# Chunk attention and a gated feed-forward layer: the order of two groups of loads, and the PSUM tiles of the wide units' values

## The chip, the core and the metric

The kernel runs on one core of one Trainium2 chip. The metric is the device time of one execution in microseconds (us). The engines meant below are PE (matmul), DVE (vector), ACT (activations and copies; its queue also issues the stores), POOL (element-wise work; its queue issues nearly all loads) and SP (a DMA queue). Each takes its own instructions strictly in the order in which they were written, and waits for the others through semaphores.

## The reference, cut to what matters

Inputs q, k, v are [8 batches, 8 heads, 576 tokens, 64]. Each 64-token chunk attends to itself; the result, taken as 4608 tokens of width 512, goes through a layer of width 2048 with a gate and back to 512.

```python
scores = (1 / sqrt(64)) * q_c @ k_c.T          # per batch, head and chunk of 64 tokens
attn = exp(scores - max(scores)); attn /= sum(attn) + 1e-9
x = (attn @ v_c)  ->  [4608, 512]
h = x @ w_in                                   # w_in: 512 x 2048
g = h * (1 / (1 + exp(-beta * h)))
out = g @ w_out                                # w_out: 2048 x 512
```

## The kernel before

**Attention, in units.** A batch has nine chunks. Batch 0 is cut into units 0 and 1 of four chunks each (the *wide* units; their loads are laid out differently) and unit 2, the last chunk alone. Every later batch has three units of three chunks: units 3, 4, 5 are batch 1, units 6, 7, 8 batch 2, and so on. For each unit: DVE transposes q and k in blocks (qt, kt; L197, L206), PE makes the scores (s, L249), DVE takes the maximum and subtracts it (mx L261, sh L270), ACT the exponential (ex L278), DVE sums and inverts (sum L289, ri L293), DVE or, from unit 7 on, POOL normalises (pn L305, L311), PE transposes the result (pt L325; from unit 9 on a DMA does) and ACT copies it out (et L333), PE multiplies by v (xa, L353; wide units L365), and ACT writes the result, transposed, into XT in SBUF (L376). For a wide unit this last copy is split: ACT takes one half (r = 0, L384), DVE the other (r = 1, L386). A wide unit's v goes through a selection on PE first (va, L218) and a copy by ACT (vv, L229).

**Feed-forward.** Tokens are taken in blocks of 512, the first three of them cut into pieces (256 + 256, 256 + 256, 320 + 192). A *hidden group* is four matmuls into one PSUM bank (hps, L399), 16 groups a piece; ACT takes the tanh (sg, L411) and DVE the gate (gt, L417). An *output group* is four matmuls with one of the four pieces of w_out (ops, L427), four groups to 128 tokens, accumulated in one bank; ACT copies the sum (osb, L437) and issues its store. A piece's hidden groups need the XT of all its tokens; output groups take the pieces of w_out in order.

**PSUM.** One two-bank tile for scores (`ps_s`), one two-bank tile for values and half of the selection (`ps_x`), and four one-bank tiles (`ps_p`) shared by hidden groups, output groups, transposes and the other half of the selection.

**Order.** A planner in the kernel writes the order of every engine's instructions. It holds a list of tasks with an engine, an estimated length, predecessors and buffers taken and given, and always emits the task that it thinks can start first, hidden and output groups with a small handicap. A task list entry says which buffers a task takes, so changing it changes the order everywhere behind it. The loads stand in a fixed order, `LOADS`, on POOL's queue; those of the third batch on follow in order of the units. A load of a batch's q, k or v (L153, L158) is eight DMAs, one per head; a "last" load (L124, L128) fetches the last chunk of batch 0, two DMAs for q, two for k and four for v; each piece of w_out is one DMA (L168). Batch 1 is loaded in two parts, its first three chunks (unit 3) and the other six (units 4 and 5). The DMAs on POOL's queue use eight semaphores in turn.

Of the kernel before, what the change touches and what calls it, by code (L numbers as in the profile page):

```python
# [8 lines left out]
FP32 = mybir.dt.float32  # L9
# [7 lines left out]
def kernel(  # L17
# [25 lines left out]
    CH = 64  # L43
    NCH = S // CH
    KDM = DM // 128
# [138 lines left out]
    sc, pr, et, xa = {}, {}, {}, {}  # L184
# [156 lines left out]
    def values(u):  # L341


        b, c0, n, grp = units[u]
        x = et.pop(u)
        a = ps_x.tile([128, 2, 512], FP32, tag="x", name="xa")
        if grp is None:
            f = raw["v", b].rearrange("p (c y s d) -> p c y s d", c=NCH, y=2, s=2)
            for c in range(n):
                for y in range(2):  # L350
                    for s in range(2):
                        for g in range(2):
                            nc.tensor.matmul(  # L353
                                out=a[64 * s:64 * s + 64, g, (y * n + c) * CH:(y * n + c + 1) * CH],
                                lhsT=f[64 * g:64 * g + 64, c0 + c, y, s, :],
                                rhs=x[64 * g:64 * g + 64, 2 * c + s, 64 * y:64 * y + 64],
                                start=True, stop=True)
        else:
            for g in range(2):
                for y in range(2):  # L360
                    for c in range(2):
                        for s in range(2):
                            for r in range(2):
                                o = ((2 * y + g) * 2 + c) * CH
                                nc.tensor.matmul(  # L365
                                    out=a[64 * s:64 * s + 64, r, o:o + CH],
                                    lhsT=tr["v", b, grp][64 * r:64 * r + 64, 2 * g + s, c, y, :],
                                    rhs=x[64 * r:64 * r + 64, 4 * g + 2 * s + c, 64 * y:64 * y + 64],
                                    start=True, stop=True)
        xa[u] = a  # L370

    def put(u, r=None):
        b, c0, n, grp = units[u]
        t0, w = b * S + c0 * CH, n * CH
        if grp is None:
            nc.scalar.activation(  # L376
                out=XT[:, :, t0:t0 + w].rearrange("p (y g) t -> p g y t", g=2),
                in_=xa.pop(u)[:, :, 0:2 * w].rearrange("p g (y t) -> p g y t", y=2),
                func=ACTF.Copy)
            return  # L380
        o = XT[:, :, t0:t0 + w].rearrange("p k (c r t) -> p k c r t", c=2, r=2)[:, :, :, r]
        i = xa[u][:, r].rearrange("p (k c t) -> p k c t", k=KDM, c=2)
        if r == 0:
            nc.scalar.activation(out=o, in_=i, func=ACTF.Copy)  # L384
        else:
            nc.vector.tensor_copy(out=o, in_=i)  # L386
# [77 lines left out]
    def task(eng, length, fn, *args, after=(), ready=0.0, take=(), give=(), lag=0.0, load=None, kind="a", behind=None):  # L464
        i = len(tasks)
        tasks.append(dict(eng=eng, len=length, fn=fn, args=args, after=[x for x in after if x is not None],
                          ready=ready, take=take, give=give, lag=lag, load=load, kind=kind, end=None))
        if behind is not None:
            order.append((behind, i))
        return i  # L470

    def dve(n):
        return 0.15 + n * 0.00105

    def act(n):
        return 0.2 + n * 0.00082
# [6 lines left out]
    AHEAD, LAZY = 9999, 1.0  # L483
    TRACE = None
    LOADS = [("k", 0, 0), ("v", 0, 0), "ident", ("q", 0, 1), ("k", 0, 1), ("v", 0, 1), ("w_in", 0), ("w_in", 1),
             ("w_out", 0), ("last", "q"), ("last", "k"), ("last", "v"), ("w_out", 1), ("w_out", 2), ("w_out", 3),
             ("q", 1), ("k", 1), ("v", 1), ("q", 1, 1, 1), ("k", 1, 1, 1), ("v", 1, 1, 1)]
    PARTS = {1: [(0, 0, 3), (1, 3, 6)]}
    PIECES = {0: [(0, 256, 0, 16), (256, 256, 0, 16)], 1: [(0, 256, 0, 16), (256, 256, 0, 16)],
              2: [(0, 320, 0, 16), (320, 192, 0, 16)]}  # L490
# [54 lines left out]
    put_of, norm_of = {}, {}  # L545
# [14 lines left out]
    for u in range(NU):  # L560
        b, c0, n, grp = units[u]
        e = n * 256
        if b > 1 and u == first[b]:
            for name in "qkv":
                for p, _, _ in PARTS.get(b, [(0, 0, 9)]):
                    pair(name, b, p)
        part = c0 // 4 if b in WIDE else max(p for p, c1, _ in PARTS.get(b, [(0, 0, 9)]) if c1 <= c0)
        for name in "qk":
            length = dve(512) if grp is not None else dve(e // 2) + 0.05
            if (b, part) == (0, 0):  # L570
                x = [task("DVE", dve(256), turn, name, 0, (i,), take=(name + "t",) if i == 0 else (),
                          after=[cast_q[i] if name == "q" else loaded["k", 0, 0]]) for i in range(2)]
                turned[name, u] = x
                last_turn[name, b] = x[1]
            else:
                x = task("DVE", length, turn, name, u, take=(name + "t",), after=[loaded[name, b, part]])
                turned[name, u] = [x]
                last_turn[name, b] = x
        if grp is not None:
            x = task("PE", 1.1, select, b, grp, after=[loaded["v", b, part], sel_in], take=("p", "p", "x"))  # L580
            copied[u] = []
            for g in range(4):
                copied[u].append(task("ACT", act(256), select_copy, b, grp, g, after=[x] + copied[u][:1],
                                      take=("vv",) if g == 0 else (), give=("x",) if g == 1 else ("p",) if g > 1 else ()))
        tq = turned["q", u] + turned["k", u]
        before = [tasks_of[u - 1]] if u else []
        length = 0.2 + 0.13 * n
        if u >= FUSE:
            w = u - LAG
            nw = units[w][2]  # L590
            x = task("PE", length + 0.02 + 0.065 * nw, lambda u=u, w=w: (values(w), scores(u)), kind="v",
                     after=tq + before + ready_for[w], take=("s", "x"), give=("qt", "kt") + values_give[w])
            value_of[w] = x
        else:
            x = task("PE", length, scores, u, after=tq + before, take=("s",), give=("qt", "kt"))
        tasks_of[u] = x
        score = x
        flips = []
        for gs in ((0,), (1,)) if u in SPLIT else ((0, 1),):
            k = len(gs)  # L600
            h = e * k // 2
            whole, start, stop = k == 2, gs[0] == 0, gs[-1] == 1
            x = task("DVE", dve(h), row_max, u, gs, after=[score])
            x = task("DVE", dve(h), shift, u, gs, after=[x], take=("sh",), give=("s",) if stop else ())
            x = task("ACT", act(h), expo, u, gs, after=[x], take=("ex",), give=("sh",))
            x = task("DVE", dve(h) + 0.23, row_sum, u, gs, after=[x])
            if u in ON_DVE:
                x = task("DVE", dve(h), norm, u, gs, nc.vector, after=[x], take=("pn",), give=("ex",))
            else:
                x = task("POOL", 0.3 + h * 0.0023, norm, u, gs, nc.gpsimd, after=[x], take=("pn",), give=("ex",))  # L610
            if u < NPE:
                x = task("PE", 0.2 + 0.06 * n * k, flip_pe, u, gs, after=[x], take=("p",), give=("pn",))
                x = task("ACT", act(h), flip_copy, u, gs, after=[x] + flips, take=("et",) if start else (), give=("p",))
            else:
                x = task("SP", 1.2, flip_dma, u, gs, after=[x], take=("et",), give=("pn",), lag=5.0)
            flips.append(x)
        ready_for[u] = flips + (copied[u] if grp is not None else [loaded["v", b, part]])
        values_give[u] = ("et", "vv") if grp is not None else ("et",)
        if u < FUSE - LAG or u >= NU - LAG:
            value_of[u] = task("PE", 0.2 + 0.065 * n, values, u, after=ready_for[u], take=("x",), give=values_give[u])  # L620
    for u in range(NU):
        b, c0, n, grp = units[u]
        if grp is None:
            put_of[u] = [task("ACT", act(n * 256), put, u, after=[value_of[u]], give=("x",))]
        else:
            y = task("DVE", dve(512), put, u, 1, after=[value_of[u]])
            put_of[u] = [y, task("ACT", act(512), put, u, 0, after=[value_of[u]], behind=y, give=("x",))]


    ms, ts, gates = [], [], {}  # L630
# [130 lines left out]
```

## Time and profile before

| | us |
|---|---|
| median of 3 runs | 318.75 (318.69 to 320.44) |
| the profiled execution | 318.93 |
| its span | 316.9 |
| PE busy | 285.8 (90%) |
| DVE busy | 207.3 (65%) |
| ACT busy | 176.0 (56%) |
| POOL busy | 161.7 (51%) |
| first matmul starts | 10.75 |

The profile is that of one execution. All times in it count from the start of its span; the execution takes 2.03 us more than the span. POOL's busy time is largely the issuing of loads, 0.56 to 0.78 us for each. The share of the span on which an engine is busy says little here, since the work changes its character: up to about 60 us loads, attention and the first feed-forward blocks start up, and from about 107 us PE has no gap of a microsecond. Waits of an engine are read from the lists of its instructions in order of time, where a bracket gives the idle time before an instruction and what ended it; a name such as `hps<-XT,w_in` gives what is written and from what.

### The profile page before, as it was taken

What the parts mean: (1) busy time and instruction counts of PE and PEld (TensorE: products, weight loads), DVE (VectorE), ACT (ScalarE), POOL (GpSimd) and SP (SyncE); (2) the same over time, 40 slices, a digit from 0 to 9 for tenths busy, and PEclk for the clock granted to TensorE, in tenths of its full rate; (3) what the DMA queues carried; (4) which work ended last, traced back from release to release, by engine and by line L of the source; (5) the groups of instructions that cost most, each with busy time, mean ns of one, the idle gap of its engine ahead of it and who ended that gap; (6) DMA issues with size and microseconds to landing.
All of it is one profiled execution on the core that took longest, in us unless ns stands there. A gap on an engine that the chain in (4) does not pass through costs nothing.

```text
span 316.9 us, 7899 instructions
## 1 busy us (share of the span) xinstructions
PE 285.8 (90%) x3254; PEld 165.0 (52%) x3254; DVE 207.3 (65%) x378; ACT 176.0 (56%) x299; POOL 161.7 (51%) x239
## 2 busy tenths in 40 slices
PE   0358787799898999999999999999999999999995
PEld 0347447376684667655455555554444444444442
DVE  3666847589898888978978888887334434334300
ACT  1337455267775777667556866667644454544511
POOL 7624389999999968899689841113000000000000
PEclk9997999999999799999999999999999999999999
DMA  6999948999999999999999963222111000001011
GB/s 100 167 212 131 204 66 71 136 137 129 175 120 155 103 63 125 165 177 131 52 199 147 134 71 85 67 64 48 43 62 41 33 33 35 33 33 68 33 66 66
DMA packets 95315, 31.54 MB, mean 100 GB/s; under 512 B 87600, under 2 KB 88880, under 8 KB 95280
## 3 DMA queue, kind: packets, MB, share of 16 engines
q0 software_dynamic: 77184, 18.12, 60.4%
q10 hardware_dynamic: 5376, 9.70, 9.1%
q1 hardware_dynamic: 12720, 3.22, 7.6%
q8 instruction: 25, 0.41, 0.6%
q14 instruction: 10, 0.08, 0.1%
HBM read 36.71 MB, written 9.44 MB: 146 GB/s over the span
## 4 chain that ended last, share of the span: by engine, by line
PE 75%; DMA 12%; POOL 7%; DVE 2%; ACT 1%; issue 1%; ACTq 0%; DVEq 0%; POOLq 0%
PE hps L399 36%; PE ops L427 35%; DMA w_out<-in_moe_w_out_dram 8%; DMA kr<-in_k_dram 3%; POOL kr L158 3%; PE s L249 3%; PE xa L353 2%; POOL qr L158 2%; POOL vr L153 2%; DVE mx L261 1%; DVE sh L270 1%; POOL w_in L163 0%; PE pt L325 0%; ACT XT L376 0%; ACT osb L437 0%
## 5 line engine op out<-in xcount | busy, mean ns | idle before, releaser
L411 ACT ACTIVATE sg<-hps,beta_sb 128x512 f32<-128x512 f32 (+3 forms) x192 | 108.5, 581 | 77.5 <-PE hps L399 74.9
L399 PE MATMUL hps<-XT,w_in 128*128 128x512 f16 (+3 forms) x768 | 145.2, 332 | 5.7 <-ACT XT L384 2.8
L417 DVE SCALAR_TENSOR_TENSOR gt<-sg,hps 128x512 f16<-128x512 f32 (+3 forms) x192 | 104.8, 551 | 69.7 <-ACT sg L411 67.9
L427 PE MATMUL ops<-w_out,gt 128*128 128x512 f16 x576 | 141.4, 379 | 0.0
L399 PEld LDWEIGHTS <-w_in 128*128 128x128 f16 x768 | 84.6, 115 | 52.7 <-issue 6.3
L427 PEld LDWEIGHTS <-gt 128*128 128x128 f16 x576 | 55.1, 98 | 59.4
L153 POOL DMA_DIRECT2D vr<-in_v_dram x64 | 45.6, 763 | 0.0
L305 POOL TENSOR_TENSOR pn<-ex,ri 128x768 f16<-128x768 f16 x17 | 25.2, 1483 | 35.2 <-ACT sg L411 15.8
L158 POOL DMA_DIRECT2D qr<-in_q_dram x64 | 38.4, 650 | 6.6 <-DMA w_out<-in_moe_w_out_dram 5.8
L158 POOL DMA_DIRECT2D kr<-in_k_dram x64 | 37.9, 623 | 1.9 <-DMA qr<-in_q_dram 1.8
L437 ACT ACTIVATE osb<-ops 128x512 f32<-128x512 f32 x36 | 21.5, 597 | 28.8 <-PE ops L427 28.4
L249 PE MATMUL s<-kt,qt 32*64 32x64 f16 x1152 | 14.6, 197 | 15.2 <-DVE kt L197 10.8
L261 DVE TENSOR_REDUCE mx<-s 128x12 f32<-128x768 f32 (+3 forms) x25 | 22.8, 914 | 7.4 <-PE s L249 7.4
L289 DVE TENSOR_REDUCE sum<-ex 128x12 f32<-128x768 f16 (+3 forms) x25 | 22.5, 901 | 4.3 <-ACT ex L278 4.2
L270 DVE TENSOR_TENSOR sh<-s,mx 128x768 f32<-128x768 f32 (+3 forms) x25 | 22.7, 911 | 0.1
L278 ACT ACTIVATE ex<-sh 128x768 f16<-128x768 f32 (+3 forms) x25 | 20.2, 814 | 2.9 <-issue 0.8
L249 PEld LDWEIGHTS <-qt 32*64 32x64 f16 x1152 | 12.1, 111 | 18.4 <-DVE qt L197 10.1
L376 ACT ACTIVATE XT<-xa 128x768 f16<-128x768 f32 (+1 forms) x22 | 17.2, 782 | 2.4 <-PE xa L353 2.0
L206 DVE STREAM_TRANSPOSE kt<-kr 128x384 f32<-128x384 f32 (+1 forms) x22 | 12.0, 544 | 4.7 <-DMA kr<-in_k_dram 2.9
L333 ACT ACTIVATE et<-pt 128x768 f16<-128x768 f16 (+3 forms) x10 | 7.3, 744 | 10.6 <-PE pt L325 10.2
L206 DVE STREAM_TRANSPOSE qt<-qr 128x384 f32<-128x384 f32 (+1 forms) x22 | 12.0, 550 | 0.4 <-DMA qr<-in_q_dram 0.4
L325 PE MATMUL pt<-ident,pn 128*128 128x128 f16 x54 | 5.3, 232 | 6.4 <-DVE pn L311 4.5
(38 smaller groups left out, 69.6 us busy)
## 6 DMA issues: line engine op xcount, KB each, us to landing
out_dram<-osb ACTq DMA_DIRECT2D x32, 256.0 KB
qr<-in_q_dram POOLq DMA_DIRECT2D x48, 72.0 KB, 4.1
kr<-in_k_dram POOLq DMA_DIRECT2D x48, 72.0 KB, 3.4
vr<-in_v_dram POOLq DMA_DIRECT2D x48, 72.0 KB, 3.3
w_in<-in_moe_w_in_dram POOLq DMA_DIRECT2D x2, 1024.0 KB, 12.4
w_out<-in_moe_w_out_dram POOLq DMA_DIRECT2D x4, 512.0 KB, 9.0
out_dram<-osb ACTq DMA_DIRECT2D x8, 128.0 KB
kr<-in_k_dram POOLq DMA_DIRECT2D x4, 128.0 KB, 7.3
```

The source lines that it names most:

```text
L153: nc.gpsimd.dma_start(out=f[p:p + 64, c0:c0 + n, y, s], in_=i.rearrange("(c p) d -> p c d", p=CH))
L158: nc.gpsimd.dma_start(out=f[p:p + 32, c0:c0 + n, x], in_=i.rearrange("(c p i) d -> p c (i d)", p=32, i=2))
L206: nc.vector.transpose(out=o, in_=f.rearrange("p (e i l) -> p e i l", i=2, l=32))
L249: nc.tensor.matmul(out=x[p0:p0 + 64, r % 2, e:e + CH], lhsT=operand("q", u, r, s, h, c), rhs=operand("k", u, r, s, h, c), start=(h == 0), ...
L261: nc.vector.tensor_reduce(out=mx[:, 0:n].rearrange("p g e o -> p g (e o)"), in_=x[:, gs[0]:gs[-1] + 1, 0:E * CH].rearrange("p g (e k) -> p ...
L270: nc.vector.tensor_tensor(out=sh, in0=x[:, gs[0]:gs[-1] + 1, 0:E * CH].rearrange("p g (e k) -> p g e k", k=CH), in1=mx[:, 0:n].broadcast_t ...
L289: nc.vector.tensor_reduce(out=sm[:, 0:n * E].rearrange("p e o -> p (e o)"), in_=ex.rearrange("p g e k -> p (g e) k"), axis=AX.X, op=ALU.add)
L305: eng.tensor_tensor(out=pn.rearrange("p e g k -> p g e k"), in0=ex, in1=rb.broadcast_to([128, m, 2 * n, CH]), op=ALU.mult)
L399: nc.tensor.matmul(out=hps[:, 0:n], lhsT=w_in16[:, kg // 2, kk, kg % 2 * 512 + i:kg % 2 * 512 + 512:4], rhs=XT[:, kk, tok0:tok0 + n], star ...
L411: nc.scalar.activation(out=sg[:, 0:n], in_=hid[j, m, a][:, 0:n], func=ACTF.Tanh, scale=beta2_sb[:, kg, i:i + 1])
L417: nc.vector.scalar_tensor_tensor(out=gt_tiles[j][:, m, a:a + n], in0=hid.pop(("s", j, m, a))[:, 0:n], scalar=1.0, in1=hid.pop((j, m, a))[: ...
L427: nc.tensor.matmul(out=o, lhsT=gt_tiles[j][:, 4 * kg + i, t * 128:t * 128 + 128], rhs=w_out16[:, kg, i, :], start=(kg == 0 and i == 0), st ...
```

## The change

Two things change. First, the values of a wide unit (`xa`) no longer go into the two-bank tile but into two one-bank tiles of the shared pool; each of the two copies out of them reads its own tile and gives it back by itself, and ACT's copy is no longer put behind DVE's. Second, the order of the loads: the eight q and eight k loads of batch 1's first three chunks, and then the last chunk's eight loads, are issued between the second and the third piece of w_out. Before, the last chunk's came between the first and second piece, and batch 1's after the fourth. Because the planner reads both, the order of instructions changes on all engines behind the first hidden groups.

```diff
 def values(u):
-        a = ps_x.tile([128, 2, 512], FP32, tag="x", name="xa")
         if grp is None:
+            a = ps_x.tile([128, 2, 512], FP32, tag="x", name="xa")
 ...
         else:
+            a = [ps_p.tile([128, 512], FP32, tag="p", name="xa") for _ in range(2)]
 ...
-                                    out=a[64 * s:64 * s + 64, r, o:o + CH],
+                                    out=a[r][64 * s:64 * s + 64, o:o + CH],
 def put(u, r=None):
-        i = xa[u][:, r].rearrange("p (k c t) -> p k c t", k=KDM, c=2)
+        i = xa[u][r].rearrange("p (k c t) -> p k c t", k=KDM, c=2)
 ...
     LOADS = [("k", 0, 0), ("v", 0, 0), "ident", ("q", 0, 1), ("k", 0, 1), ("v", 0, 1), ("w_in", 0), ("w_in", 1),
-             ("w_out", 0), ("last", "q"), ("last", "k"), ("last", "v"), ("w_out", 1), ("w_out", 2), ("w_out", 3),
-             ("q", 1), ("k", 1), ("v", 1), ("q", 1, 1, 1), ("k", 1, 1, 1), ("v", 1, 1, 1)]
+             ("w_out", 0), ("w_out", 1), ("q", 1), ("k", 1), ("last", "q"), ("last", "k"), ("last", "v"),
+             ("w_out", 2), ("w_out", 3), ("v", 1), ("q", 1, 1, 1), ("k", 1, 1, 1), ("v", 1, 1, 1)]
 ...
         if u < FUSE - LAG or u >= NU - LAG:
-            value_of[u] = task("PE", 0.2 + 0.065 * n, values, u, after=ready_for[u], take=("x",), give=values_give[u])
+            value_of[u] = task("PE", 0.2 + 0.065 * n, values, u, after=ready_for[u],
+                               take=("x",) if grp is None else ("p", "p"), give=values_give[u])
 ...
-            y = task("DVE", dve(512), put, u, 1, after=[value_of[u]])
-            put_of[u] = [y, task("ACT", act(512), put, u, 0, after=[value_of[u]], behind=y, give=("x",))]
+            y = task("DVE", dve(512), put, u, 1, after=[value_of[u]], give=("p",))
+            put_of[u] = [y, task("ACT", act(512), put, u, 0, after=[value_of[u]], give=("p",))]
```

## Prediction

> **What bounds the kernel now.** I read the page's table of slices first, then the chain of work that ended last, then POOL's queue in order of time, then the waits of ACT and PE, and last the granted clock in 2 us windows. The profiled execution took 318.93 us, a span of 316.9 and 2.03 around it; the median is 0.18 lower. All sums are made in the profiled execution, and 0.18 comes off at the end.
>
> PE's row of the slices is full from the tenth slice on, but not before. PE is idle for 16.8 us between its first matmul (10.75) and its last, nearly all of it before 103. What can be won lies there. The page's sum of the chain, then the same chain in order of time (start, length, what):
>
> ```profile
> PE 75%; DMA 12%; POOL 7%; DVE 2%; ACT 1%; issue 1%; ACTq 0%; DVEq 0%; POOLq 0%
> ```
> ```profile
> 12.31 16.01 DMA w_out<-in_moe_w_out_dram
> ...
> 30.29 10.00 DMA w_out<-in_moe_w_out_dram
> ...
> 41.14 4.42 POOL kr L158 x8
> 45.56 4.93 POOL vr L153 x8
> 50.49 4.47 POOL qr L158 x8
> 54.95 3.82 POOL kr L158 x7
> 58.77 3.12 DMA kr<-in_k_dram
> ```
>
> See that from 28 to 62 the chain is not on PE: it is POOL, which issues one small load after another at 0.56 to 0.62 us each. POOL's queue shows why it starts so late (start, length, what; in brackets the idle time before it and who ended it):
>
> ```profile
> 34.55 0.56 POOL L158 DMA_DIRECT2D qr<-in_q_dram  x1 [0.94 <-DMA w_out<-in_moe_w_out_dram]
> 38.04 0.56 POOL L158 DMA_DIRECT2D qr<-in_q_dram  x1 [2.93 <-DMA w_out<-in_moe_w_out_dram]
> 40.58 0.56 POOL L158 DMA_DIRECT2D qr<-in_q_dram  x1 [1.98 <-DMA w_out<-in_moe_w_out_dram]
> ```
>
> Counting POOL's loads from its first, each waits for the one **eight places ahead** of it: these are loads 30, 31 and 32, and loads 22, 23 and 24 are the last three pieces of w_out. Loads 19, 20 and 21 stop likewise for w_in (until 21.16 and 26.15) and the first w_out (28.61). The order of loads therefore decides where POOL stands still.
>
> **Part one, the values tiles.** In the kernel before, ACT's copy of a wide unit waits for DVE's copy of the other half:
>
> ```profile
> 23.60 0.60 ACT L384 ACTIVATE XT<-xa 128x512 f16<-128x512 f32 x1 [1.33 <-DVE XT L386]
> ...
> 39.79 0.60 ACT L384 ACTIVATE XT<-xa 128x512 f16<-128x512 f32 x1 [1.63 <-DVE XT L386]
> ```
>
> Both read one tile; in the changed kernel's instructions ACT's copy waits for PE alone. For unit 0 the hidden-layer matmuls can then start when DVE's copy ends, 23.57, and not at 24.25: 0.65 us earlier, and so for all up to 36. The values may start up to 0.5 us later (their bank is freed by the copies ending at 22.27, not 21.72), hidden behind DVE's maximum, which runs to 22.98. No instruction is added. The two tiles are held in a pool of four that the hidden layer uses too, but only until the copies end. The 0.65 comes to nothing below, since the next stop is set by POOL.
>
> **Part two, the loads.** I replay POOL's queue with its own durations. w_out piece 1 issues at 12.9. The first four q loads of batch 1 follow by 16.6 (the wide v wait until 16.06 stays). The fifth, sixth and seventh stop at 21.16, 26.15 and 28.61, as their places did before. The eighth waits for piece 1, which lands 2.4 to 3.45 us after piece 0 (28.3; the spacings of large loads here: 25.9 to 28.3, 34.3 to 37.75 to 40.3), plus 0.28 to release: it issues at 31.0 to 32.0. Then eight k loads, nothing stopping them: the last starts 8 x 0.55 later, 35.4 to 36.4. Before, that k load started at 45.0 and DVE turned k at 48.66, 3.66 later; so now **k can be turned at 39.0 to 40.0, some 9 us earlier**.
>
> The price stands behind it on POOL: the last chunk's eight loads (2 x 0.70, 2 x 0.67, 4 x 0.60) end at 41.1 to 42.1 and were done by 29.2 before. Its k lands near 41.5, and w_out pieces 2 and 3 issue at about 41.6 and 42.2 instead of 29.7 and 30.3. Piece 1 took 5.1 from issue to landing behind a like handful of small loads, so piece 2 lands at 46.7 (46.2 to 47.2), piece 3 at 49.7 (48.8 to 50.6), against 37.75 and 40.3. The lower end, from the 2.0 us that the quickest small load takes plus 2.4 of transfer, is 45.5 and 47.9. I take the row, which is the same kind of load. The Trainium skill (DMA: Bandwidth & Descriptors, Anatomy of one DMA) fits 2.0 us plus bytes at 436 GB/s, an estimated 4.4 us for the 1 MB that a piece reads; the trace's own quickest piece is slower. By the page the sum would be some 0.7 us lower.
>
> Now PE, from the built order. The first two output groups (0.86 each; piece 1 is there) and the transposes of unit 1 end at 36.5, ACT's copy at 37.5, the values of unit 1 at 38.0. DVE's queue, however, has batch 1's k transpose and the last chunk's q transpose **ahead of unit 1's copy**: 39.5 + 0.58 + 0.30 + 0.68 gives 41.1, where it ended at 39.76 before. PE idles some 3.1 us there. Then one hidden group (0.44), a wait of 0.4 for the last chunk's k, its scores (0.3), seven hidden groups to 45.6, and a wait to 46.7 for piece 2; output group 0.86, two hidden groups, and the scores of unit 3 end at 49.1 (49.86 before); a wait of 0.65 for piece 3, and 11.5 us of work (32 + 4 output matmuls at 0.216, 24 hidden at 0.11, transposes and values 1.0), to 61.1.
>
> The scores of unit 4 need the second half of batch 1's q and k. On POOL, v's seventh load waits for piece 2 (47.0), its eighth for piece 3 (50.0), and ends at 50.6; before, 50.49. So q and k come no earlier, and these scores start at about 62.7 as before (62.65), PE idle for 1.6. By then PE has done two output groups less (1.73) and unit 3's transposes and values more (0.7). **This stretch costs 1.1 us**: the q and k that came 9 us earlier are paid for by weights and v that come later.
>
> **What follows, 62 to 107.** Here the order pays. Before, the third block had to wait for unit 7's normalisation on POOL, queued behind eight loads, and for ACT's copy of unit 6; then PE ran at half clock (columns of the second fence: window, its length, PE busy, granted clock, DMA share, GB/s):
>
> ```profile
> 102.36 0.51 PE L325 MATMUL pt<-ident,pn 128*128 128x128 f16 x6 [1.25 <-POOL pn L305]
> 103.16 1.12 PE L399 MATMUL hps<-XT,w_in 128*128 128x320 f16 x4 [0.29 <-ACT XT L376]
> ```
> ```profile
> 26.00:28.00 2.00, 2.00 (x12) 0.50 1.23 156
> ...
> 104.00:106.00 2.00, 2.00 (x10) 0.50 0.68 70
> ```
>
> Twenty matmuls took 4.55 there; the 24 at 110.97 took 3.45, so 2.88 would do: 1.7 lost. In the changed order unit 8's scores precede the end of the second block, unit 7's normalisation stands behind two loads of that batch instead of eight (about 97.7 done instead of 102.3, needed near 99.8), and ACT has only a flip copy (0.81) ahead of unit 6's. So 1.25 + 0.29 + 1.7 = 3.2 should go. Other waits in the stretch (0.26, 0.63, 0.56, 0.37) I keep, and add 0.9 because DVE gets tight: it is busy for 35.8 of the 40 us from 64 to 104, and for 7.80 of 8 at its fullest:
>
> ```profile
> 88.00:96.00 8.00, 8.00 (x64) 6.09 (x62) 7.80 (x18) 5.06 (x13) 8.00 (x13) 1.00 1.50 117
> ```
>
> This stretch gives **-2.3** (the columns are PE, PEld, DVE, ACT, POOL busy). From 107 PE is full in both. Sum: 318.93 + 1.1 - 2.3 = 317.7, less 0.18: **317.5 us**.
>
> **Rivals.** (1) The weights land early: at 45.5 and 47.9, v's loads stop less, unit 4's scores start at 60.9, and PE's waits for w_out shrink. The stretch gives -0.8 instead of +1.1: 315.6, or 314.7 if the 0.9 goes too; with no stop on POOL at all (landing by 44 and 46) 313.3. For it: the transfer alone is 2.4. Against: every piece behind small loads took 5 us or more.
>
> (2) The change doesn't do what it says in the end: 9 us earlier q and k buy nothing, since POOL's later loads are where they were, and the third block's stop returns in other places. 318.75 + 1.1 = 319.8.
>
> (3) Slower: DVE's queue has all four transposes of batch 2's units 6 and 7 in one place, behind unit 5's normalisation. They wait for batch 2's last k load: second-half v, q, k of 8 loads each put it at about 77.3. If DVE arrives before 75.5, gates stand behind the wait, PE runs dry and its clock halves. Price: 3.3 for the wait and 1.9 for the half clock (the first half-clock stretch: 60 matmuls took 8.5, at 0.11 they need 6.6), which turns the -2.3 into +2.9: 318.75 + 1.1 + 2.9 = 322.8. I reckon that DVE arrives near 78, so it is unlikely.
>
> A word on the clock, for (3): the two half-clock stretches last 3.4 us and begin after waits of only 2.04, and of 1.25 and 0.29 us with small matmuls between, while one of 2.06 at 47 had no such result. The Trainium skill (TensorE: Matmul & The Clock Gate, HAM oscillation) warns of idle gaps above about 3.4 us, judged over free-running windows. By that rule a window that holds little but the new gap of 3.1 near 38 halves the clock for the groups behind it, some 1.6 us, of which 1.1 would fall into the wait for piece 2; the sum would be 0.5 higher.
>
> **How the numbers follow.** Forecast 0.45 (its own range 316 to 319), rival 1 0.22, rival 2 0.20, rival 3 0.13. The range leaves out rival 3 and the far end of rival 1: **313.8 to 320.9**. One per cent, 3.2 us, is about what a measurement of this kernel can tell from no change. Below 315.6: half of rival 1 and more, and the forecast's tail, 0.24; above 321.9: 0.12; between: 0.64.
>
> **What would show it.** Right: k of unit 3 turned near 39.5; the scores of unit 3 only some 1 us earlier; w_out waits of PE at about 46 and 49; unit 4's scores within 1 us of 62.7; no half clock near 103. Wrong: pieces 2 and 3 landed before 45, or a DVE wait for batch 2's k near 75.

## The result, and the profile after

The changed kernel takes 320.28 us (median of 20 runs, 318.53 to 321.76), the kernel before 319.07 in the same set. The ratio is **1.0044, 95% interval 1.0024 to 1.0064**: about 1.4 us slower (1.2 by the two medians), where 1.2 us faster was forecast. The ratio goes by the fast runs alone, and three of the twenty of the kernel before are over 1.5% above its fastest. The time is inside the forecast's range, on the wrong side of no change.

Line numbers of the changed kernel are two higher from the values on (hidden groups L401, output groups L429, wide copies L386 and L388). The profiled execution took 321.76 us, a span of 320.0. It is the slowest of its set, and some 0.9 us of that are lost early: POOL waits 5.29 us for w_in at its place 20, against 4.35 to 4.41 in the kernel before and in nine of the eleven experiments (5.39 and 5.07 in the other two, loads alone and the second filler). All three long waits are under the new order of loads, which also has seven short ones; whether it has a part in them is open. So stops are compared by their length below, and a time of this profile stands about 0.9 late.

The page's row of the granted clock (40 equal slices, in tenths), and the sum of the chain:

```profile
PEclk9999959959999999999999999999999999999999
```
```profile
PE 74%; DMA 13%; POOL 6%; DVE 4%; issue 1%; ACT 1%; ACTq 0%; DVEq 0%; POOLq 0%
```

The chain is still made of DMA and POOL up to the 65th microsecond. The two 5s in the clock's row are new, at 40 to 48 and at 64 to 72. In order of time, from 30 to 65 (start, length, what):

```profile
32.76 4.44 POOL kr L158 x8
...
42.85 7.40 DMA w_out<-in_moe_w_out_dram
...
53.42 5.51 DMA qr<-in_q_dram
...
59.21 1.67 POOL kr L158 x3
60.89 1.10 issue
61.99 0.55 POOL kr L158
62.53 2.05 DMA vr<-in_v_dram
64.59 0.58 DVE kt L206
```

The eight k loads that ran from 41.14 to 45.56 run from 32.76 now. But the last of the second set of k loads, the ones for unit 4, starts at 61.99. On POOL's queue (start, length, what, idle time before it) the stops have moved from before those k loads to behind them:

```profile
47.91 0.63 POOL L153 DMA_DIRECT2D vr<-in_v_dram  x1 [0.78 <-DMA w_out<-in_moe_w_out_dram]
50.53 0.63 POOL L153 DMA_DIRECT2D vr<-in_v_dram  x1 [2.00 <-DMA w_out<-in_moe_w_out_dram]
...
59.21 1.67 POOL L158 DMA_DIRECT2D kr<-in_k_dram  x3 [1.37 <-DMA qr<-in_q_dram]
61.99 0.56 POOL L158 DMA_DIRECT2D kr<-in_k_dram  x1 [1.10 <-issue]
```

The first two were forecast. The last two, 2.5 us together, were not: a q load that takes 5.51 us from issue to landing, and a stop that the profile puts down to nothing it shows. On PE there are two long stops, the second of them behind these k loads:

```profile
42.09 1.04 PE L401 MATMUL hps<-XT,w_in 128*128 128x256 f16 x4 [4.52 <-DVE XT L388]
...
65.21 0.85 PE L249 MATMUL s<-kt,qt 32*64 32x64 f16 x48 [3.62 <-DVE kt L206]
65.99 1.89 PE L429 MATMUL ops<-w_out,gt 128*128 128x512 f16 x4
```

The first stop is a wait for DVE's copy of unit 1. On DVE the last chunk's q transpose stands ahead of this copy, and it waits for its load:

```profile
39.01 0.58 DVE L206 STREAM_TRANSPOSE kt<-kr 128x384 f32<-128x384 f32 x1 [2.73 <-DMA kr<-in_k_dram]
41.15 0.31 DVE L206 STREAM_TRANSPOSE qt<-qr 128x128 f32<-128x128 f32 x1 [1.57 <-DMA qr<-in_q_dram]
41.39 0.65 DVE L388 CAST XT<-xa 128x512 f16<-128x512 f32 x1
```

The four output matmuls behind the second stop take 1.89 us, where four alone take 1.03 elsewhere. The windows say why (window, its length; PE, PEld, DVE, ACT and POOL busy; granted clock, DMA share, GB/s):

```profile
42.00:44.00 2.00, 1.91 (x23) 1.18 (x24) 0.67 (x3) 0.48 (x1) 2.00 (x4) 0.50 0.65 40
...
66.00:68.00 2.00, 2.00 (x12) 0.82 (x7) 1.86 (x2) 0.08 (x1) 2.00 (x4) 0.50 1.19 75
...
104.00:106.00 2.00, 2.00 (x35) 1.09 (x35) 2.00 (x5) 0.07 (x1) 2.00 (x3) 1.00 0.36 135
```

Read by seconds, the clock is 0.50 from 40.2 to 47.0 and from 64.1 to 71.0: twice 6.8 us. The profile of the kernel before has it twice for 3.4 us (24.8 to 28.2 and 103.3 to 106.7); neither is there now. From both profiles, all in us:

| stretch | PE idle before | PE idle after | half clock before | half clock after |
|---|---|---|---|---|
| 0 to 24 | 16.48 | 15.40 | 0 | 0 |
| 24 to 38 | 2.47 | 3.12 | 3.4 | 0 |
| 38 to 66 | 5.39 | 7.78 | 0 | 8.7 |
| 66 to 110 | 3.21 | 1.14 | 3.4 | 5.0 |
| whole span: idle | 31.1 | 31.3 | | |
| whole span: PE busy | 285.8 | 288.7 | | |

**The waits of PE add up to the same.** The change moves 2.4 us of idle time into 38 to 66 and takes 2.1 us out of 66 to 110. The two kernels have the same 3254 matmuls, and PE is busy 2.9 us longer with them. Nearly all of the difference of the profiles, 2.9 of 3.1 us of span, is slower matmuls, not longer waiting. That made the clock the first suspect.

### The profile page after: what moved, and what is told of

Same layout as the page of the kernel before. It is cut to its first block, busy times and chain, and to the rows that moved or that the text cites. A ratio compares the mean times of both kernels' runs of the same rounds, so it can differ in the third digit from the quotient of the medians.

```text
span 320.0 us, 7910 instructions
## 1 busy us (share of the span) xinstructions
PE 288.7 (90%) x3254; PEld 166.5 (52%) x3254; DVE 206.3 (64%) x378; ACT 177.3 (55%) x299; POOL 162.1 (51%) x239
## 4 chain that ended last, share of the span: by engine, by line
PE 74%; DMA 13%; POOL 6%; DVE 4%; issue 1%; ACT 1%; ACTq 0%; DVEq 0%; POOLq 0%
PE ops L429 36%; PE hps L401 33%; DMA w_out<-in_moe_w_out_dram 8%; PE s L249 3%; DMA kr<-in_k_dram 2%; POOL kr L158 2%; PE xa L353 2%; DVE gt L419 2%; DMA qr<-in_q_dram 2%; POOL qr L158 1%; DVE sum L289 1%; POOL vr L124 1%; DMA vr<-in_v_dram 1%; ACT sg L413 1%; DVE sh L270 1%
## 5 line engine op out<-in xcount | busy, mean ns | idle before, releaser
L401 PE MATMUL hps<-XT,w_in 128*128 128x512 f16 (+3 forms) x768 | 149.1, 334 | 8.6 <-DVE XT L388 6.0
L429 PE MATMUL ops<-w_out,gt 128*128 128x512 f16 x576 | 144.9, 383 | 0.1
L401 PEld LDWEIGHTS <-w_in 128*128 128x128 f16 x768 | 84.7, 116 | 57.6 <-issue 5.3
L429 PEld LDWEIGHTS <-gt 128*128 128x128 f16 x576 | 55.7, 98 | 59.5 <-issue 1.4
L158 POOL DMA_DIRECT2D qr<-in_q_dram x64 | 38.4, 643 | 14.3 <-DMA w_in<-in_moe_w_in_dram 9.7
L305 POOL TENSOR_TENSOR pn<-ex,ri 128x768 f16<-128x768 f16 x17 | 24.9, 1472 | 31.1 <-DVE ri L293 19.9
L249 PE MATMUL s<-kt,qt 32*64 32x64 f16 x1152 | 15.4, 202 | 13.9 <-DVE kt L197 10.1
L353 PEld LDWEIGHTS <-vr 64*64 64x64 f16 x512 | 5.8, 108 | 7.9 <-issue 7.4
```

Source lines behind the costliest of these rows:

```text
L158: nc.gpsimd.dma_start(out=f[p:p + 32, c0:c0 + n, x], in_=i.rearrange("(c p i) d -> p c (i d)", p=32, i=2))
L249: nc.tensor.matmul(out=x[p0:p0 + 64, r % 2, e:e + CH], lhsT=operand("q", u, r, s, h, c), rhs=operand("k", u, r, s, h, c), start=(h == 0), ...
L305: eng.tensor_tensor(out=pn.rearrange("p e g k -> p g e k"), in0=ex, in1=rb.broadcast_to([128, m, 2 * n, CH]), op=ALU.mult)
L401: nc.tensor.matmul(out=hps[:, 0:n], lhsT=w_in16[:, kg // 2, kk, kg % 2 * 512 + i:kg % 2 * 512 + 512:4], rhs=XT[:, kk, tok0:tok0 + n], star ...
L429: nc.tensor.matmul(out=o, lhsT=gt_tiles[j][:, 4 * kg + i, t * 128:t * 128 + 128], rhs=w_out16[:, kg, i, :], start=(kg == 0 and i == 0), st ...
```

## The experiments

All times are medians beside the kernel before, run on the same chip in the same set. Its median was 318.99 us in the set of the first four experiments, 318.77 for the next four, 319.23 for the ninth, 319.94 for the last two. Differences in us are worked out from the ratio, times 319; their intervals are about 1 us to either side.

### Each half alone

Theory: the cost lies in the loads, and the tiles do nothing. Rival: the tiles' earlier start disturbs the planner's order behind it. The first kernel has the new tiles with the old list of loads:

```diff
-             ("w_out", 0), ("w_out", 1), ("q", 1), ("k", 1), ("last", "q"), ("last", "k"), ("last", "v"),
-             ("w_out", 2), ("w_out", 3), ("v", 1), ...
+             ("w_out", 0), ("last", "q"), ("last", "k"), ("last", "v"), ("w_out", 1), ("w_out", 2), ("w_out", 3),
+             ("q", 1), ("k", 1), ("v", 1), ...
```

> Part one alone: the two one-bank tiles with the old order of loads; PE's order is then that of the kernel before but for a few instructions at its end. Clock theory (the change loses through two new stops of PE, at 38 to 42 and at 61.6 to 65.2 us, each of which leaves PE at half clock for some 6.6 us): no new stop, so no loss; the hidden layer starts 0.65 us earlier and POOL's loads swallow it; 318.4 to 319.1, ratio to before 0.998 to 1.000. Weights theory (it loses because pieces 2 and 3 of w_out land 10 us later): the same. If the tiles themselves cost something, slower than 319.1.

Measured: 318.96 us, ratio 1.0009 (0.9978 to 1.0041). The copies no longer wait for each other; in this kernel and in the changed one ACT's second copy waits for PE alone:

```profile
37.62 0.60 ACT L386 ACTIVATE XT<-xa 128x512 f16<-128x512 f32 x1 [0.55 <-PE xa L367]
```

And it buys nothing that these runs can tell. The second kernel has the new loads with the old two-bank tile:

```diff
-            a = [ps_p.tile([128, 512], FP32, tag="p", name="xa") for _ in range(2)]
+            a = ps_x.tile([128, 2, 512], FP32, tag="x", name="xa")
```

> Part two alone: the new order of loads with the old two-bank tile; the order on PE, DVE and POOL is that of the changed kernel. Clock theory and weights theory alike: the whole loss is here, ratio to before 1.002 to 1.008, k of unit 3 turned near 39, stops of PE before the first hidden group of the second piece and before unit 4's scores, half clock behind both. If the loss needs both parts, 1.000.

Measured: 319.55 us, 1.0021 (0.9988 to 1.0053). This alone is not apart from either kernel, but its profile shows the changed kernel's two stops (3.32 and 3.44 us) and two half-clock stretches behind them (43.2 to 46.6 and 63.7 to 70.5). With the tiles alone neither stop is there (PE's longest between 30 and 72 is 2.50, at 45 to 48). The loads make them.

### Keeping the clock up

Theory: the half clock behind the two stops is what costs. Rival: the later weights and loads cost by the stops themselves, whatever the clock. The test puts useless matmuls into the two stops, which changes no load and no other order:

```diff
+    FILL = {1: 18, 3: 11}
...
         xa[u] = a
+        if u in FILL:
+            z = ps_x.tile([128, 2, 512], FP32, tag="x", name="fill")
+            for i in range(FILL[u]):
+                nc.tensor.matmul(out=z[:, i % 2, :], lhsT=w_in16[:, 0, 0, 0:128], rhs=w_in16[:, 0, 1, 0:512],
+                                 start=True, stop=True)
```

> The changed kernel plus 18 matmuls of 512 columns after unit 1's values and 11 after unit 3's, into a bank nobody reads: they fill the two stops and keep PE busy, while every wait stays where it is. Clock theory: full clock behind both stops. Behind the first, 0.8 us at most is won, since piece 2 of w_out lands at 47.6 anyway; behind the second, matmuls between 65.2 and 71.5 took some 2.9 us more than at full clock, and that goes: about 317.4, ratio to before 0.994 to 0.997. Weights theory, or any by which the clock is beside the point: 320.3 or a little more, ratio 1.004.

Measured: **318.13 us**, 0.9974 (0.9947 to 1.0001), 2.2 us less than the changed kernel by the ratios, and their intervals don't overlap. That is just above the clock theory's range (0.994 to 0.997) and far from the rival's 1.004. The fillers sit in the stops, and what follows runs at the full clock (the second fence is the same windows as above):

```profile
35.70 4.06 PE L377 MATMUL fill<-w_in 128*128 128x512 f16 x18
40.98 0.63 PE L407 MATMUL hps<-XT,w_in 128*128 128x256 f16 x4 [1.22 <-DVE XT L394]
...
46.61 1.02 PE L435 MATMUL ops<-w_out,gt 128*128 128x512 f16 x4 [0.89 <-DMA w_out<-in_moe_w_out_dram]
...
49.25 1.02 PE L435 MATMUL ops<-w_out,gt 128*128 128x512 f16 x4 [0.23 <-DMA w_out<-in_moe_w_out_dram]
...
60.92 2.53 PE L377 MATMUL fill<-w_in 128*128 128x512 f16 x11 [0.92 <-ACT XT L384]
63.43 0.57 PE L250 MATMUL s<-kt,qt 32*64 32x64 f16 x48
```
```profile
42.00:44.00 2.00, 1.85 (x17) 1.69 (x16) 1.70 (x5) 1.47 (x4) 2.00 (x4) 1.00 0.75 77
66.00:68.00 2.00, 2.00 (x58) 1.33 (x57) 1.50 (x4) 0.62 (x2) 2.00 (x5) 1.00 1.01 121
```

With the clock up, PE reaches the weights before they land, and the two waits for w_out that the forecast named appear at 46.61 and 49.25. In the changed kernel the slow matmuls before them hide these waits: part of the first half-clock stretch is free. One filler at a time shows how the cost is shared.

```diff
-    FILL = {1: 18, 3: 11}
+    FILL = {1: 18}          # the first kernel
+    FILL = {3: 11}          # the second kernel
```

> The changed kernel with 18 matmuls of 128x512 of no use added behind unit 1's values alone (the stop before the first hidden group of unit 1's tokens); the stop before unit 4's scores is left as it is. Against the kernel before (319.0 in the last set). Clock theory, both stops cost by half clock: half of the 2.15 us that both fillers brought, 319.2 (ratio 1.000 to 1.002), and no half clock between 40 and 48 but still one from about 64 to 71. Clock theory, with the half clock of the first stop falling into the waits for w_out that follow it: nothing, 320.3 (1.003 to 1.005).

> The changed kernel with 11 matmuls of 128x512 of no use added behind unit 3's values alone (the stop before unit 4's scores); the first stop is left as it is. If both stops cost by half clock: 319.2 (1.000 to 1.002). If the first stop's half clock falls into the waits for w_out: all of the gain of both fillers, 318.1 (0.996 to 0.999), with half clock from about 41 to 47 only.

Measured: 319.72 us, 1.0025 (0.9993 to 1.0057), with the first filler, and 318.58, 1.0002 (0.9979 to 1.0025), with the second. Against the changed kernel's 1.0044 that is 0.6 us for the first and 1.3 for the second. The second value is what "both stops cost" foresaw, the first lies between its two cases; the intervals overlap, so that both stops cost, the second more, is likely and not shown. Each kernel's profile has half clock only behind the stop that was not filled.

The last filler asks what the kernel before pays for its own half clock at 103:

```diff
     def scores(u):
...
+        if u == 9:
+            z = ps_p.tile([128, 512], FP32, tag="p", name="fill")
+            for i in range(5):
+                nc.tensor.matmul(out=z, lhsT=w_in16[:, 0, 0, 0:128], rhs=w_in16[:, 0, 1, 0:512],
+                                 start=True, stop=True)
```

> The kernel before with 5 matmuls of 128x512 of no use behind unit 9's scores, in PE's wait of 1.25 us for POOL's normalisation at 101; they add nothing to the matmuls on the path if they end by 102.4. If that wait makes the half clock from 103.4 to 106.8: that is gone, and the time is 1.7 us lower, 317.3 (0.994 to 0.996); then the change gains nothing at equal clock (its kernel with fillers took 318.1). If the half clock has another cause: 319.0 (0.999 to 1.001), and at equal clock the change is worth the 0.9 us by which its kernel with fillers lies under the kernel before.

Measured: 317.56 us, 0.9977 (0.9944 to 1.0009), between the two cases. The stop of 1.25 us and the half clock behind it are gone from its profile:

```profile
101.90 1.25 PE L259 MATMUL fill<-w_in 128*128 128x512 f16 x5
103.04 0.51 PE L330 MATMUL pt<-ident,pn 128*128 128x128 f16 x6
104.02 1.25 PE L404 MATMUL hps<-XT,w_in 128*128 128x320 f16 x8 [0.47 <-ACT XT L381]
```

But a profile is one run. The mean granted clock was recorded for every run of the experiments and of the changed kernel, and it gives an estimate of each run's half-clock time: twice what the clock lacks to 1, times the span, since the clock is 0.50 where it is lowered (0.989 in the profile of the kernel before gives 7.0 us, for the 6.8 read by seconds).

| kernel | runs | half clock, mean us |
|---|---|---|
| before, in the experiments' sets (one run of 388 us left out) | 97 | 5.9 |
| changed | 20 | 12.3 |
| changed, both fillers | 12 | 1.3 |
| changed, first filler | 12 | 4.6 |
| changed, second filler | 12 | 7.2 |
| before, with its filler | 12 | 5.8 |

**The changed kernel has twice the half clock of the kernel before in its runs, and both fillers take nearly all of it away and 2.2 us with it.** That is shown: no load was moved, and unit 4's scores start at 63.43 with both fillers and at 63.78 with the first alone, so the second stop ends where it did. The first filler takes away more half clock than the second and less time, which again says that part of the first stretch is free.

The filler of the kernel before did not do the same. Its profiled run, at a clock of 1.000, is one of only two such among twelve; the mean half clock is that of the kernel without the filler. Its seven runs at 0.993 or more took 316.59 to 317.96 us, its five at 0.989 or less 319.23 to 320.43. So its median says nothing of the half clock at 103 alone, and what the kernel before pays for that is not measured. Nor do any two of these kernels stand side by side at equal clock. The nearest that the record has: six runs of the kernel before at 0.997 or more, with its filler or without, have a median of 316.9, ten of the changed kernel with both fillers at 0.998 or more one of 318.1. This hints that at full clock the new order is about 1 us slower; but the six were picked by their clock, and the two groups come from two chips.

### Where the stops come from

First guess: the first stop ends when the last chunk's small loads have landed, and POOL's later stops come from w_out's last pieces. Then these pieces ahead of the last chunk's loads, with every other engine's order kept, should help. In the kernel a written-out list of tasks takes the planner's place; put as a list of loads, the edit is:

```diff
-             ("w_out", 0), ("w_out", 1), ("q", 1), ("k", 1), ("last", "q"), ("last", "k"), ("last", "v"),
-             ("w_out", 2), ("w_out", 3), ("v", 1), ...
+             ("w_out", 0), ("w_out", 1), ("q", 1), ("k", 1), ("w_out", 2), ("w_out", 3),
+             ("last", "q"), ("last", "k"), ("last", "v"), ("v", 1), ...   # order of PE, DVE, ACT as in the changed kernel
```

> The changed kernel with every engine's order held as it is, but pieces 2 and 3 of w_out issued before the last chunk's eight loads instead of after them. They issue near 37.2 and land near 42.5 and 45.5 instead of 47.6 and 50.2; the last chunk's k comes 2 us later (first stop longer by about that). Clock theory and weights theory: v's two waits of 0.8 and 2.0 us on POOL go, so unit 4's scores start at 62.4 instead of 65.2 and the second stop shrinks below 1 us. By the clock theory its half clock goes too, so 2.8 + 2.9 in all, less what the longer first stop costs: 315.5 to 317.5. By the weights theory alone 2.8: 317.5 to 318. If neither matters (the planner's new order is to blame): 320.3.

Measured: 319.62 us, 1.0027 (1.0000 to 1.0054). The expectation was missed. The second stop is gone, but the first grew from 4.5 to 7.5 us, with half clock from 39.5 to 49.8:

```profile
46.47 1.04 PE L401 MATMUL hps<-XT,w_in 128*128 128x256 f16 x4 [7.51 <-DVE XT L388]
```

The last chunk's q now lands behind the weights (DVE waits 6.58 us for it), and DVE's copy of unit 1 stands behind its transpose. Time moved from one stop into the other. Next, the written order itself: unit 1's DVE copy ahead of those transposes, and the work that needs only early weights drawn forward. Again the kernel holds a written-out list of tasks; in words:

```diff
   DVE:
-  turn q 3, turn k 3, turn q 2, copy of unit 1, turn k 2, gates ...
+  copy of unit 1, 4 gates (pipelined), turn q 3, turn k 3, turn q 2, gates, turn k 2, ...
   PE:
-  hidden groups of block 0's second piece mixed with output groups of pieces 2 and 3, scores of unit 4, then block 1
+  all hidden groups of that piece, output groups of pieces 0 and 1, then 2 and 3; 11 hidden groups of block 1, scores of unit 4
```

> The changed kernel's loads and tiles with another written order: unit 1's DVE copy ahead of the transposes of q and k of unit 3 and the last chunk; all 16 hidden groups of block 0's second piece and the output groups with w_out pieces 0 and 1 ahead of those with piece 2; 11 hidden groups of block 1's first piece ahead of unit 4's scores. If the stops at 38 and 61 come from an order of PE and DVE that doesn't fit the new landing times: no stop over 1.5 us between 37 and 64, no half clock in 40 to 48 and 64 to 71, and 2 to 5 us less than the changed kernel: 315.3 to 318.3 (0.988 to 0.998). If they come from the loads themselves (the weights' bytes and POOL's issues): the stops only move, and the time stays within 1 us of the changed kernel's 320.3 (1.001 to 1.007).

Measured: **324.59 us**, 1.0178 (1.0141 to 1.0215). Both expectations were missed. The first stop went as the order theory has it, but DVE now had block 1's gates ahead of unit 4's transposes, and a new stop came at 79 with half clock from 81 to 88:

```profile
38.30 3.87 PE L401 MATMUL hps<-XT,w_in 128*128 128x256 f16 x28 [0.83 <-DVE XT L388]
...
73.83 0.57 PE L249 MATMUL s<-kt,qt 32*64 32x64 f16 x48 [1.55 <-DVE kt L206]
...
82.73 0.82 PE L325 MATMUL pt<-ident,pn 128*128 128x128 f16 x6 [3.87 <-DVE pn L305]
```

Much of the loss is waiting: from 66 to 110 PE idles 8.7 us here, against 1.1 in the changed kernel. To see whether only that placing was bad, unit 4 was put first again (in words, as above):

```diff
-  3 gates of block 1, turn q 4, turn q 5, 8 gates, turn k 4, turn k 5, scores of unit 4 and its softmax
+  turn q 4, turn q 5, turn k 4, turn k 5, scores of unit 4 and its softmax, then block 1's gates,
+  with block 0's last output groups between them
```

> The written order of the reordered kernel (324.6) mended at one place: the transposes of q and k of units 4 and 5, unit 4's scores and its softmax stand ahead of block 1's hidden groups on DVE and PE, with output groups of block 0 between them. In the reordered kernel the two stops of the changed kernel were gone, but q's transposes of unit 4 stood behind three gate products of block 1 (66.55) and k's behind eight more (73.19), so that its scores came at 73.83 and the next stop of 3.87 at 78.9 with half clock behind it. If that placing alone made it slow: unit 4's scores at 63 to 65, no stop over 2 us from 37 to 84, no half clock there, and 313 to 317 (ratio 0.982 to 0.995), under both kernels. If the second batch's values come too late whatever the order (PE has too little work from 37 to 84): a stop of 3 us or more is left somewhere in that stretch, and the time is 319 to 323 (1.000 to 1.013).

Measured: 323.27 us, 1.0172 (1.0124 to 1.0219), with a profiled span of 321.5. That is above even the second theory's range by a little, and its sign is that theory's: PE comes to unit 4 early and waits there, at the same time as in the changed kernel:

```profile
36.73 3.86 PE L401 MATMUL hps<-XT,w_in 128*128 128x256 f16 x28 [0.83 <-DVE XT L388]
...
65.63 0.85 PE L249 MATMUL s<-kt,qt 32*64 32x64 f16 x48 [4.61 <-DVE kt L206]
```

So the first stop is made by DVE's written order, which puts the copy behind the wait for the last chunk's q (4.5 us become 0.83 when the copy stands first, and 7.5 when that q lands later). Drawing work forward left the second stop longer, 4.61 for 3.62. Both orders were written by hand and have further waits of their own, so their totals say nothing finer. The last question was whether unit 4's k sets the second stop. One edit brings it earlier:

```diff
-             ("w_out", 2), ("w_out", 3), ("v", 1), ("q", 1, 1, 1), ("k", 1, 1, 1), ("v", 1, 1, 1)]
+             ("w_out", 2), ("w_out", 3), ("q", 1, 1, 1), ("k", 1, 1, 1), ("v", 1), ("v", 1, 1, 1)]
```

> The changed kernel with one edit in its list of loads: the second part of batch 1's q and k (units 4 and 5) stands ahead of v of batch 1's first part; the planner writes the order from it. In the changed kernel the stop of 3.6 us before unit 4's scores stayed through two other written orders, and unit 4's k was turned at 64.6 and 65.0. If the arrival of k sets that stop: k is issued some 4 us earlier, unit 4's scores come at 59 to 62, the stop and the half clock behind it (1.7 us by the fillers) go, and the time is 316.5 to 318.9 (ratio 0.993 to 1.000), unless v becomes late in its place. If v becomes late: PE waits for v's loads at unit 3's values by 2 us or more, half clock stays in 60 to 72, and the time is 319.5 to 322 (1.002 to 1.010).

> The kernel with k ahead of v, and 18 matmuls of 128x512 of no use behind unit 1's values, which keep the clock up through the first stop. If k's arrival made the second stop and its half clock: no half clock at all between 36 and 76 and 0.5 to 0.9 us less than without the filler: 316 to 318 (0.990 to 0.998), at or under the changed kernel with both fillers (318.1). If v is late instead: half clock stays in 60 to 72, and the time is 318.8 to 321.5.

Measured: 319.60 us, 1.0017 (0.9986 to 1.0047), and with the first stop's filler 319.30, 0.9993 (0.9960 to 1.0025). Of the first kernel, on PE:

```profile
59.33 0.58 PE L249 MATMUL s<-kt,qt 32*64 32x64 f16 x48
...
61.30 0.21 PE L353 MATMUL xa<-et,vr 64*64 64x64 f16 x1 [1.24 <-DMA vr<-in_v_dram]
...
62.83 0.55 PE L353 MATMUL xa<-et,vr 64*64 64x64 f16 x19 [1.32 <-DMA vr<-in_v_dram]
```

Unit 4's scores come at 59.33 without a wait, so k's arrival did set that stop. But v takes its place: 1.24 + 1.32 us at unit 3's values, with half clock from 63.7 to 67.1 behind them. The expectations' second case is what happened, if at the low edge of its range, and the filled kernel shows the same (half clock from 62.7 to 66.2). POOL has a fixed number of small loads to issue one by one, and each of these two orders leaves another of them last. None of the eleven kernels is shown to beat the kernel before; the lowest medians are those of the kernel before with its filler and of the changed one with both.

## Why the prediction was wrong

- **Part one, the values tiles** ("comes to nothing below"): right. The tiles alone give 1.0009.
- **k of unit 3 turned at 39.0 to 40.0**: right by luck, 39.01 in a profile that stands 0.9 late. In the experiments with the same q and k loads and no such delay (both fillers, the first filler, w_out earlier, k ahead of v) it is turned at 37.8 to 38.4, 0.6 to 1.2 us before that range.
- **PE idle some 3.1 near 38, since DVE's copy of unit 1 stands behind two transposes**: the mechanism was right, and putting the copy first took the stop away. The size was not: 4.52 us in the changed kernel, where the copy ended at 42.04 and not at 41.1 and PE came to it at 37.6 and not at 38.0. Without the profile's lateness it is 3.66 (k ahead of v). The sum 39.5 + 0.58 + 0.30 + 0.68 has no wait for the last chunk's q, and DVE waits 1.57 us for it in both of these profiles. With k ahead of v the copy ends at 40.9, near the forecast, only because k is turned earlier.
- **Weights at 46.7 and 49.7, with waits of PE at about 46 and 49**: the weights were right (about 47.6 and 50.25, in a profile that stands late; 46.6 and 49.2 with both fillers). The waits did not show in the changed kernel because half clock covered them; with the clock up they are there, 0.89 at 46.61 and 0.23 at 49.25.
- **"q and k come no earlier, and these scores start at about 62.7"**: this is the first step that failed. The forecast let POOL issue the second set of q and k from 50.6 on without a stop, as before. The trace shows two stops more, 1.37 and 1.10 us (the first comes in some profiles only, the second, at 0.99 to 1.21, in all with these loads and this order of work), and the scores came at 65.21, 63.4 to 65.2 in the four experiments with the same loads and order. PE's stop was 3.62 us and not 1.6.
- **"This stretch costs 1.1 us"** carried the second and larger failure: no term for the clock. Half clock behind the new stops was put at nothing in the sum; the two fillers together show it to cost 2.2 us. The aside gave the rule's price for the first stop as 0.5 higher, and the first filler's 0.6 is near it. The aside left out the second stop, forecast at 1.6, and its half clock is the dearer one, 1.3 by its filler. Unlike the first it is followed by no wait that could hide it.
- **62 to 107, -2.3**: the parts that were to go went. There is no stop before the third block's transposes and no half clock at 103 in the profile. The 0.9 for a tight DVE did not come: from 66 to 110 PE idles 2.1 us less than before. But the half clock that the second stop starts reaches to 71 and takes back some of that. The 1.7 for the half clock at 103 was taken from one profile; no run isolates it.

With the missing term the forecast's own sum is -1.2 + 2.2 = +1.0 us, where 1.2 to 1.4 were measured. The clock behind the new stops is thus enough to turn the sign. That the rest fits is not shown: it leans on the 1.7, and at equal clock the prediction's other terms come to +1.1 - 1.54 + 0.9 = +0.5 us, for which the runs at full clock give only the hint above, about 1 us.

Rival 2 (the earlier q and k buy nothing, and the stops return elsewhere, 319.8) is nearest to what happened, in mechanism and in time; it lacked the clock as well. Rival 3's wait of DVE for batch 2 near 75 did not occur, nor did the weights land early as in rival 1.

The Trainium skill (TensorE: Matmul & The Clock Gate, HAM oscillation) names idle gaps above about 3.4 us as what throttles PE. The stops of 4.52 and 3.62 us here agree with it, and by that rule a second stop of the forecast 1.6 is safe. The traces say that this is no safe bound: half clock also followed 1.25 and 0.29 us with short matmuls around them (the kernel before, at 101 to 103), and 1.24 and 1.32 us (k ahead of v, at 60 to 63).

What stays open: the stop of about 1.1 us on POOL before the last k load, put down to "issue". It is there, at 0.99 to 1.21, in the changed kernel and in the five experiments that keep its loads and order (w_out earlier among them), not in the kernel before nor before the same load of the two reordered ones. Ahead of a v load it is there too when k stands before v (0.84, and 0.25 with the filler). The planner counts room in a ring for the loads in flight (`RING`); whether the queue had run out of such room there was not tested. No run told the cause.

## What to carry to other kernels

Price a stop of the matmul engine by its length and by what runs after it: look whether a wait that must come anyway hides the slow matmuls, as at 47, or full work follows, as at 65. When idle time and instructions are the same in two profiles and the busy time is not, read the granted clock before looking for a wait, and read it for all runs: the profiled run of the kernel before with its filler had full clock, and most of its other runs had not. And where one engine issues many small loads in turn, moving some forward makes others last: follow the queue to the end of the batch, with a margin for flights that take longer, before counting the earlier ones as won.

## What the runs showed of the hardware beyond this

The half clock came in steps. Its lengths, from the seconds of each trace: about 3.4 us (the kernel before twice; tiles alone twice; after 1.24 + 1.32, and after 1.31 + 0.31 with the filler; loads alone, first stop of 3.32; the second stop of 3.7 with only the first filled), 6.8 us (stops of 3.62 and 4.52 in the changed kernel, 3.66 with k ahead of v, 3.87 in the reordered kernel, 4.61 with unit 4's scores first, 3.44 with the loads alone) and 10 us (stops of 5.83 and 7.51). The same stop can give one step or two: 3.62 gave 6.8 us, 3.7 gave 3.4. And the step does not always start where a stop ends: in the kernel before one covers the first hidden groups from 24.8, and in two experiments that begin the same way the records show none there. So a single profile is one draw of this. How wide the draw is, the 97 runs of the kernel before show: the mean clock lies between 0.979 and 1.000, and the 19 runs at 0.995 or more have a median of 317.86 us, the 16 at 0.984 or less one of 321.39.
